# Decode of four attention layers: six blocks of output-weight rows laid out unevenly over the partitions

## The chip, the cores and the metric

The kernel runs on one core of a Trainium2 chip. The metric is the time of one execution in microseconds on the device; the median of three runs before the change is 1974.63 us (1973.94 to 1975.71).

## The reference

One token goes through four layers, A, B, A, B. Each layer normalises the token, makes a query of 32 heads of 192 from it, attends over a cache of 8192 keys and values a head, and projects the 32 x 192 = 6144 results back to 640 with the output weights `wo`, whose result is added to the token.

```python
def _A_ref(x, k_cache, v_cache, wq, wo):        # _B_ref is the same with its own arrays
    q = ((x @ wq).reshape(B, Sq, Hq, Dh)).transpose(0, 2, 1, 3)
    scores = jnp.einsum("bhqd,bhkd->bhqk", q, k) * (Dh ** -0.5)
    p = _softmax(scores, axis=-1)
    o = jnp.einsum("bhqk,bhkd->bhqd", p, v)
    return o.transpose(0, 2, 1, 3).reshape(B, Sq, Hq * Dh) @ wo
x = A_x
x = x + _A_ref(_layernorm(x), A_k_cache, A_v_cache, A_wq, A_wo)
x = x + _B_ref(_layernorm(x), B_k_cache, B_v_cache, B_wq, B_wo)
x = x + _A_ref(_layernorm(x), A_k_cache, A_v_cache, A_wq, A_wo)
x = x + _B_ref(_layernorm(x), B_k_cache, B_v_cache, B_wq, B_wo)
```

## The kernel before

The kernel reads 845 MB, nearly all of it caches, and reads the caches once for each layer. Layers are counted from 0 here (layers 0 and 2 are A, 1 and 3 are B). A layer's 32 heads are taken as 16 pairs. The keys of a pair, and its values, are 6.29 MB each: one head on 64 partitions, the other on the other 64, 49,152 bytes a partition. They land in halves or whole in a pool of eight slots (`slot`, line 129).

For a pair the order of the work is: VectorE multiplies the keys in place by the query (line 744), TensorE sums the products with matmuls against the identity (lines 72, 762), VectorE and ScalarE make the softmax (802 to 817), TensorE multiplies by the values (859, 72), and `gather` (869) picks each head's row out of the result: VectorE 883 and 885, a matmul (899), and two ScalarE copies with the softmax's divisor (908) into `orow`, one row of SBUF on one partition.

**A block of output weights** belongs to five pairs (`PAIRS_W`): 5 x 384 = 1920 of the 6144 rows of `wo`, 640 wide, 1280 bytes a row. `transfer` (line 439) loads it with one transfer of 128 partitions with `NW` = 15 consecutive rows each (lines 492, 493). A layer has three such blocks, called (layer, 0), (layer, 1), (layer, 2) here, and one more pair's rows at its end. After the fifth pair of a block:

- `columns` (718) turns `orow` from a row into 15 columns of 128: column i takes every 15th element from i on, with a one-row matmul into `TB` (722), and one ScalarE copy puts the columns into `oT` (725).
- `project_row` (688) multiplies: for each of the 15 columns, two matmuls, one for each half of the 640 outputs, with the column as weights (695). They add up in one accumulator (`YR`). Its last matmul is what frees the block's slot (`freed[n]`).

**The order.** `steps` is the order of the work, `plan` that of the loads (lines 262 to 324). All loads are issued by SyncE in the order of `plan`; `before` names whose work must be done before a load may overwrite a slot, and `transfer` waits for these (`free`). A load that has to wait holds up all that follow it on SyncE. `ahead` (504) hands SyncE the loads whose conditions are known. In layers 0 and 1, places are fixed: the block has the third slot of a ring, which keys of a later pair use next. In layers 2 and 3 `allot` (357) gives each load the slots that come free first; in layer 2 the values of the pair after a block get one of their halves in the block's slot, so this half's issue waits for the end of `project_row`. A transfer's end is a semaphore that counts to 16, one for each DMA engine.

Of the kernel before, what the change touches and what calls it, by code (L numbers as in the profile page):

```python
# [4 lines left out]
ACT = mybir.ActivationFunctionType  # L5
# [77 lines left out]
def build(nc, A_x, A_k, A_v, A_wq, A_wo, B_x, B_k, B_v, B_wq, B_wo, out):  # L83
# [21 lines left out]
    OI = PD // P  # L105
    WB = [[], [6], [], [7]]
    NB = [sum(b) for b in WB]
    VLAST = [0, 2, 0, 4]
    G = 4
    VK = 8  # L110
# [6 lines left out]
    with ExitStack() as ctx:  # L117
# [311 lines left out]
        def block_rows(l, i=None):  # L429
# [3 lines left out]
            x = 0 if l != 1 else TS // 2 if i is None else -(NW - NB[l]) * D  # L433
            return t[:, x + a * D:x + b * D], a, b

        def quarters(n):
            return n[0] == "v" and n[2:] == (NPAIR - 1, 1) and NB[n[1]] > 0

        def transfer(n):
            l = n[1]  # L440
            o = ORDER[l]
            w = W[l % 2]
            free = [freed[b] for b in before[n]]
            if n[0] in ("wol", "woe"):
                r0 = o["wol"] * PD
                a, b = (0, OI) if l < 3 else (0, OI - 1) if n[0] == "wol" else (OI - 1, OI)
                return SP.op(lambda s: s.dma_start(
                    last_rows(l)[:, a * D:b * D], w["wo"][r0:r0 + PD].rearrange("(p i) n -> p (i n)", p=P)[:, a * D:b * D]),
                    *free, sem=semOL if n[0] == "wol" else semOE, inc=16)
            if n[0] == "wob":  # L450
                r0 = o["wo"][2] * PD
                t, a, b = block_rows(*n[1:])
                return SP.op(lambda s: s.dma_start(
                    t, w["wo"][r0:r0 + PAIRS_W * PD].rearrange("(p i) n -> p (i n)", p=P)[:, a * D:b * D]),
                    sem=(semOB, semOE)[n[2]], inc=16)
            if n[0] == "vq":
                n = ("v", l, NPAIR - 1, 1)
            if n[0] in ("kh", "kp"):
                h = 2 * pair(l, 0)
                i = n[3] if n[0] == "kp" else 0  # L460
                a, b, to = PIECE[i]
                r = w["k"][0, h:h + 2].rearrange("h (p j) d -> (h p) (j d)", j=J)[:, a:b]
                return SP.op(lambda s: s.dma_start(to, r), *free, sem=[semVQ, *semR, semS[A_WQ]][i], inc=16)
            i = place[n]
            t = slot[i]
            if n[0] in "kv":
                h = 2 * pair(l, n[2])
                r = w[n[0]][0, h:h + 2].rearrange("h (p j) d -> (h p) (j d)", j=J)
                if quarters(n):
                    x = TS - VLAST[l] * TS // 8  # L470
                    if n in landed:
                        return SP.op(lambda s: s.dma_start(t[:, x:], r[:, TS + x:]), sem=semVQ, inc=16)
                    return SP.op(lambda s: s.dma_start(t[:, 0:x], r[:, TS:TS + x]), *free, sem=semS[i], inc=16)
                if whole(*n[:3]):
                    if n[3] == 1:
                        return landed[n[:3] + (0,)]
                    f = lambda s: s.dma_start(pool[:, i * TS:(i + 2) * TS], r)
                else:
                    x = TS // 2 if n == ("k", 0, 0, 0) else 0
                    f = lambda s: s.dma_start(t[:, x:], r[:, n[3] * TS + x:(n[3] + 1) * TS])  # L480
            elif n[0] == "wq" and l < 2:
                a, b = (0, DC) if l == 0 else (0, DC - 1) if n[2] == 0 else (DC - 1, DC)
                f = lambda s: s.dma_start(pool[:, i * TS:i * TS + (b - a) * QW],
                                          w["wq"].rearrange("(p c) n -> p (c n)", c=DC)[:, a * QW:b * QW])
            elif n[0] == "wq":
                c0, k = Q_PARTS[n[2]]
                f = lambda s: s.dma_start(
                    wq_rows(l, n[2]),
                    w["wq"][:, o["q1"] * PD:o["q1"] * PD + QC[l]].rearrange("(p c) n -> p c n", c=DC)[:, c0:c0 + k, :])
            else:  # L490
                r0 = o["wo"][n[2]] * PD
                t, _, k = block_rows(l) if n[2] == 2 else (t[:, 0:NW * D], 0, NW)
                f = lambda s: s.dma_start(t, w["wo"][r0:r0 + PAIRS_W * PD].rearrange("(p i) n -> p (i n)", p=P)[:, 0:k * D])
            return SP.op(f, *free, sem=semS[i], inc=16)

        def need(n):
# [51 lines left out]
        def layer(l, ev_z, ev_true):  # L548
# [139 lines left out]
            def project_row(n, w, o, ev_o):  # L688

                t3 = w.rearrange("p (i n) -> p i n", n=D)  # L690
                k = t3.shape[1]
                PE.wait(ev_o, need(n), last["YB"])
                for i in range(k):
                    for h in range(2):
                        e = PE.op(lambda t, i=i, h=h, f=l < 3 and n[2] == 0 and i == 0, fin=n == last_row and i == k - 1: t.matmul(  # L695
                            YR[32 * h:32 * h + 1, :], lhsT=o[:, i:i + 1], rhs=t3[:, i, h * HD:(h + 1) * HD], start=f, stop=fin,
                            skip_group_check=True), signal=(i == k - 1 and h == 1), bank=YBu)
# [17 lines left out]
                y_first[0] = False  # L715
                return e

            def columns(k):

                PE.wait(last["row_written"], last["TT"], ev_const)  # L720
                for i in range(k):
                    e = PE.op(lambda t, i=i: t.matmul(TB[:, i:i + 1], lhsT=orow[:, i:k * P:k], rhs=one_b[96:97, :],
                                                      start=True, stop=True), signal=(i == k - 1), bank=TBu)
                last["orow"] = freed[n] = e
                last["TT"] = AC.op(lambda a: a.activation(oT[:, 0:k], TB[:, 0:k], ACT.Copy),  # L725
                                   e, last["oT"], bank=TBu)

            ev_S, ev_s, ev_p, ev_O, ev_l = {}, {}, {}, {}, {}

# [139 lines left out]
            def gather(p):  # L869
# [31 lines left out]
                if end:  # L901
                    last["TTn"] = last["TO"] = AC.op(
                        lambda a: a.activation(oTl[:], TB[:, 0:OI], ACT.Copy, scale=rl[:, 0:1]), e, ev_rl, last["oTl"], bank=TBu)
                else:
                    o0 = (pair(l, p) - ORDER[l]["wo"][p // PAIRS_W]) * PD
                    AC.wait(e, ev_rl, last["orow"], last["qbc"])
                    for h in range(2):
                        last["TO"] = last["row_written"] = AC.op(lambda a, h=h: a.activation(  # L908
                            orow[:, o0 + h * DH:o0 + (h + 1) * DH], TB[64 + 32 * h:65 + 32 * h, C_O:C_O + DH], ACT.Copy,
                            scale=rl[64 + 32 * h:65 + 32 * h, h:h + 1]), bank=TBu)  # L910

            q_ready = False
            for n in [n for n in steps if n[1] == l]:
# [22 lines left out]
                    q_rows(n[2])  # L936
                    q_ready = n[2] == 2 or q_ready
                elif n[0] == "wc":
                    columns(NW)
                    last["oTw"] = last["TT"]  # L940
                elif n[0] == "wo":
                    t, _, k = block_rows(l) if n[2] == 2 else (slot[place[n]][:, 0:NW * D], 0, NW)
# [95 lines left out]
```

## Time and profile before

| | |
|---|---|
| median of three runs | 1974.63 us |
| span of the profiled execution, first to last instruction | 1972.3 us |
| read from HBM | 845.22 MB, 429 GB/s over the span |
| mean granted TensorE clock | 0.842 |
| DMA issues of a block (line 493) | 12, of 1.3 to 2.5 MB, 15.9 to 38.4 us from issue to landing |
| issue and last landing of the six blocks that change, us | (0,0) 148.16, 174.74; (0,1) 299.40, 326.13; (1,1) 804.24, 830.64; (2,0) 1144.18, 1161.94; (2,1) 1297.18, 1313.64; (3,0) 1602.01, 1635.30 |

Times within the execution count from its first instruction. The profile's page gives, for each engine, its busy time and share of the span; a row of 40 digits shows the busy share in 40 equal slices, 9 for 90% or more. "q1" is the queue of the loads that SyncE issues; "q8" and "q14" bring the program's instructions. The chain of waits goes back from an instruction to what released it; in it, a line has start, duration, and what ran. In the timeline a line has start, duration, engine, line of the kernel, what it writes and reads, and in brackets how long the engine had been idle and what ended that.

### The profile page before, as it was taken

How to read it: one execution, taken by the hardware profiler on the slowest of the kernel's cores; microseconds unless marked ns; L12 is line 12 of the kernel's file. 1: busy time of each engine (PE TensorE's matmuls, PEld its weight loads, DVE VectorE, ACT ScalarE, POOL GpSimd, SP SyncE). 2: the span in 40 equal slices, each digit the busy share in tenths (PEclk: the TensorE clock that was granted, in tenths of full speed). 3: DMA queues.
4: the chain of work that ended last, by engine and by line, in shares of the span. 5: the costliest groups of instructions: out<-in, count | busy, mean ns of one | idle time of the engine just before them, and what ended most of it. 6: DMA issues, size and time to landing. Idle time of an engine off the chain costs nothing.

```text
span 1972.3 us, 13138 instructions
## 1 busy us (share of the span) xinstructions
PE 1425.8 (72%) x8648; PEld 138.3 (7%) x2789; DVE 1204.7 (61%) x910; ACT 146.2 (7%) x465; POOL 4.6 (0%) x25
## 2 busy tenths in 40 slices
PE   4788777886578888788786675776676667657658
PEld 0000000000200100000020000000002001000001
DVE  3566665667256566665856565665664765665756
ACT  0000000000000000000000000000000100000000
POOL 0000000000000000000000000000000000000000
PEclk9898998998689888988887777777787878777779
DMA  9999999999999999999999999999999999999998
GB/s 414 430 431 432 431 434 431 436 425 427 437 429 431 430 428 432 433 429 432 431 419 436 426 430 434 429 431 430 431 430 427 433 432 436 432 433 432 431 432 369
DMA packets 27245, 846.07 MB, mean 429 GB/s; under 512 B 3122, under 2 KB 3252, under 8 KB 4148
## 3 DMA queue, kind: packets, MB, share of 16 engines
q1 hardware_dynamic: 27044, 845.23, 99.7%
q8 instruction: 45, 0.74, 0.2%
q14 instruction: 12, 0.10, 0.0%
q10 hardware_dynamic: 144, 0.00, 0.0%
HBM read 845.22 MB, written 0.00 MB: 429 GB/s over the span
## 4 chain that ended last, share of the span: by engine, by line
DMA 58%; PE 22%; DVE 19%; ACT 1%; issue 0%; SPq 0%
DMA pool<-in_B_k_cache_dram 24%; DMA pool<-in_A_v_cache_dram 16%; DMA pool<-in_A_k_cache_dram 16%; DVE pool L744 14%; PE S L72 13%; PE OY L72 4%; PE OY L859 3%; DMA pool<-in_B_wo_dram 2%; DVE OY L883 1%; DVE acc L885 1%; DVE s_sb L802 1%; DMA pool<-in_B_v_cache_dram 1%; PE OY L695 1%; ACT p_sb L817 1%; DVE pool L776 1%
## 5 line engine op out<-in xcount | busy, mean ns | idle before, releaser
L744 DVE TENSOR_TENSOR pool<-pool,q_sb 128x3584 bf16<-128x3584 bf16 (+3 forms) x460 | 844.4, 1907 | 189.5 <-DMA pool<-in_B_k_cache_dram 99.1
L72 PE MATMUL S<-pool,ident 128*128 128x512 bf16 x3004 | 758.8, 407 | 37.9 <-DVE pool L744 34.5
L883 DVE TENSOR_TENSOR OY<-OY,small 128x1536 f32<-128x1536 f32 x60 | 106.0, 1767 | 253.4 <-PE OY L72 253.2
L72 PE MATMUL OY<-pool,p_sb 128*16 128x512 bf16 x1920 | 211.9, 530 | 0.0
L72 PE MATMUL S<-ident 128*128 128x512 bf16 x775 | 185.3, 387 | 0.0
L859 PE MATMUL OY<-pool,p_sb 128*16 128x512 bf16 (+1 forms) x1216 | 148.0, 510 | 42.0 <-DMA pool<-in_A_v_cache_dram 34.6
L802 DVE TENSOR_REDUCE s_sb<-S 128x128 f32<-128x1024 f32 x63 | 77.2, 1225 | 110.4 <-PE S L72 110.4
L899 PE MATMUL TB<-acc,small 128*33 128x192 f32 x120 | 39.8, 423 | 135.6 <-DVE acc L885 135.6
L885 DVE TENSOR_REDUCE acc<-OY 128x192 f32<-128x1536 f32 x60 | 105.5, 1758 | 2.0
L762 PE MATMUL S<-pool,ident 128*128 128x512 bf16 x66 | 33.7, 511 | 95.8 <-DVE pool L744 95.8
L908 ACT ACTIVATE rows<-TB,small 1x192 bf16<-1x192 f32 x120 | 49.5, 412 | 571.4 <-PE TB L899 569.9
L589 ACT ACTIVATE q_sb<-QM 128x192 bf16<-128x192 f32 x59 | 19.5, 330 | 928.9 <-PE QM L645 928.9
L807 PE MATMUL QM<-ident,m_bf 128*64 128x64 bf16 x128 | 14.0, 216 | 86.4 <-DVE m_bf L804 86.4
L817 ACT ACTIVATE p_sb<-s_sb,small 64x128 bf16<-64x128 f32 x128 | 55.7, 435 | 194.4 <-DVE small L811 193.6
L832 PE MATMUL TB<-small,ones 128*33 128x2 f32 x120 | 14.4, 190 | 74.1 <-ACT p_sb L817 74.1
L873 DVE RECIPROCAL small<-TB 33x2 f32<-33x2 f32 x64 | 11.2, 175 | 88.9 <-PE TB L832 72.6
L645 PEld LDWEIGHTS QM<-rows,one_b 1*64 1x64 bf16 x118 | 6.1, 100 | 720.5 <-issue 720.5
L859 PEld LDWEIGHTS OY<-pool,p_sb 128*16 128x16 bf16 (+1 forms) x1216 | 36.3, 110 | 199.0 <-issue 148.0
L530 PE MATMUL S<-ident 128*128 128x512 bf16 x80 | 33.8, 422 | 17.2 <-DMA pool<-in_A_k_cache_dram 10.9
L695 PE MATMUL OY<-pool,oT 128*1 128x320 bf16 x330 | 38.1, 408 | 2.4 <-ACT oT L725 2.2
L811 DVE TENSOR_REDUCE small<-QM 128x1 f32<-128x64 f32 x64 | 14.4, 225 | 31.3 <-PE QM L807 31.3
L899 PEld LDWEIGHTS TB<-acc,small 128*33 128x33 f32 x120 | 9.6, 124 | 272.3 <-DVE acc L885 272.3
(87 smaller groups left out, 270.2 us busy)
## 6 DMA issues: line engine op xcount, KB each, us to landing
pool<-in_B_v_cache_dram SPq DMA_DIRECT2D x28, 6144.0 KB, 27.6
pool<-in_A_v_cache_dram SPq DMA_DIRECT2D x27, 6144.0 KB, 23.8
pool<-in_B_k_cache_dram SPq DMA_DIRECT2D x27, 6144.0 KB, 22.2
pool<-in_A_k_cache_dram SPq DMA_DIRECT2D x35, 3072.0 KB, 19.9
pool<-in_A_k_cache_dram SPq DMA_DIRECT2D x13, 6144.0 KB, 21.0
pool<-in_A_v_cache_dram SPq DMA_DIRECT2D x10, 3072.0 KB, 13.5
pool<-in_B_k_cache_dram SPq DMA_DIRECT2D x10, 3072.0 KB, 20.3
pool<-in_A_wo_dram SPq DMA_DIRECT2D x6, 2400.0 KB, 18.4
```

The costliest lines, as they stand in the source:

```text
L72: return t.add_instruction(mybir.InstMatmult(name=t.bass.get_next_instruction_name(), engine=mybir.EngineType.PE, ins=[t.lower_ap(rhs), t. ...
L530: t.matmul(SP_[0][:, :], lhsT=ident[:], rhs=ident[:].unsqueeze(1).broadcast_to([P, 4, P]), start=True, stop=True)
L695: e = PE.op(lambda t, i=i, h=h, f=l < 3 and n[2] == 0 and i == 0, fin=n == last_row and i == k - 1: t.matmul(YR[32 * h:32 * h + 1, :], lhs ...
L744: e = DV.op(lambda v, d0=d0, QD=QD, kin=kin, kout=kout, n=n: v.tensor_tensor(kout[:, :, d0:d0 + QD], kin[:, :, d0:d0 + QD], q_sb[qi][:, d0 ...
L762: t.matmul(S[:, :], lhsT=ident[:], rhs=k3[:, :, d0:d0 + R], start=d0 == 0, stop=fin)),
L802: lambda v: v.tensor_reduce(s[:], S_[:].rearrange("p (j r) -> p j r", r=R), AX.X, ALU.add),
L817: ev_p[p] = AC.op(lambda a, h=h, r=r: a.activation(p_sb[par][r, :, h], s[r, :], ACT.Exp, bias=negm[par][r, 0:1], accum_out=l_col[par][r, h ...
L859: t.matmul(o, lhsT=x, rhs=y, start=f, stop=fin) if c == 0 else
L883: e = DV.op(lambda v: v.tensor_tensor(o3, o3, pick[:, 0:VK].unsqueeze(2).broadcast_to([P, VK, DH]), ALU.mult), bank=Ou)
L885: e = DV.op(lambda v: v.tensor_reduce(acc[:], O.rearrange("p (i d) -> p d i", d=DH), AX.X, ALU.add), e, bank=Ou)
L899: e = PE.op(lambda t: t.matmul(TB[64:97, C_O:C_O + DH], lhsT=half33, rhs=acc[:], start=True, stop=True), bank=TBu)
L908: last["TO"] = last["row_written"] = AC.op(lambda a, h=h: a.activation(orow[:, o0 + h * DH:o0 + (h + 1) * DH], TB[64 + 32 * h:65 + 32 * h, ...
```

## The change

Six blocks, (0,0), (0,1), (1,1), (2,0), (2,1) and (3,0), are laid out in another way; the other six stay. Of the block's 1920 rows, the first 128 x 14 = 1792 go to the 128 partitions, 14 consecutive rows each, with one transfer. The last 128 rows go to 32 partitions, four consecutive rows each: partitions 0 to 15 and 32 to 47, with two further transfers of 16 partitions. The change takes partitions 0 to 3 and 32 to 35 for those of DMA engine 0, the next four each for those of engine 1, and so on to engine 3; the source of each of the two transfers is led by a dimension of four, one step an engine, with the engine's four partitions inside it. All three transfers count on the slot's semaphore, and the last one's event is the block's.

The rest follows the layout. `orow` holds the last 128 results in the order of the partitions (the copy of the block's last head is cut in two, the second with a permuting pattern). `columns` makes 14 columns of 128 and, for each of the two groups of partitions, four columns of 16; three copies take them to `oT`, which is 18 wide. `project_row` runs over 14 columns on all partitions, then four on partitions 0 to 15, then four on 32 to 47: 22 pairs of matmuls in the place of 15, with a wait for its own earlier matmuls before the third part.

```diff
+    UNEVEN = {(l, b): (14, ((4, 4),)) for l, b in ((0, 0), (0, 1), (1, 1), (2, 0), (2, 1), (3, 0))}
...
-        oT = sb("oT", [P, NW], BF16)
+        oT = sb("oT", [P, NW + 3], BF16)
...
+        def uneven(l, b):
+
+            m, groups = UNEVEN.get((l, b), (NW, ()))
+            r, c, out = P * m, m, []
+            for k, x in groups:
+                out.append((r, c, k, x))
+                r, c = r + 8 * k * x, c + x
+            assert r == PAIRS_W * PD
+            return m, out, c
...
+                if n[1:] in UNEVEN:
+                    m, groups, _ = uneven(*n[1:])
+                    e = SP.op(lambda s: s.dma_start(t[:, 0:m * D], rows_of[0:P * m].rearrange("(p i) n -> p (i n)", p=P)),
+                              *free, sem=semS[i], inc=16)
+                    for r, c, k, x in groups:
+                        for h in range(2):
+                            to = t[32 * h:32 * h + 4 * k, c * D:(c + x) * D]
+                            r4 = rows_of[r:r + 8 * k * x].rearrange("(b a i) n -> b a i n", b=4, i=x)[:, h * k:(h + 1) * k]
+                            e = SP.op(lambda s, to=to, r4=r4: s.dma_start(to, r4.rearrange("b a i n -> a b (i n)")), sem=semS[i], inc=16)
+                    return e
...
             def project_row(n, w, o, ev_o):
...
+                todo = [(slice(0, P), i) for i in range(t3.shape[1])]
+                if n[0] == "wo" and n[1:] in UNEVEN:
+                    m, groups, _ = uneven(*n[1:])
+                    todo = todo[:m] + [(slice(32 * g, 32 * g + 4 * k), i) for g in range(2) for _, c, k, x in groups for i in range(c, c + x)]
                 PE.wait(ev_o, need(n), last["YB"])
-                for i in range(k):
+                for j, (a, i) in enumerate(todo):
+                    end = j + 1 == len(todo) or a.start < todo[j + 1][0].start
+                    if a.start and not todo[j - 1][0].start:
+                        PE.wait(e)
                     for h in range(2):
...
-                            YR[32 * h:32 * h + 1, :], lhsT=o[:, i:i + 1], rhs=t3[:, i, h * HD:(h + 1) * HD], start=f, stop=fin,
-                            skip_group_check=True), signal=(i == k - 1 and h == 1), bank=YBu)
+                            YR[32 * h:32 * h + 1, :], lhsT=o[a, i:i + 1], rhs=t3[a, i, h * HD:(h + 1) * HD], start=f, stop=fin,
+                            skip_group_check=True), signal=end and h == 1, bank=YBu)
...
-            def columns(k):
+            def columns(b):
 
+                m, groups, k = uneven(l, b)
+                todo = [(slice(0, P), i, orow[:, i:m * P:m]) for i in range(m)]
+                for r, c, ke, x in groups:
+                    for g in range(2):
+                        a = r + 4 * g * ke * x
+                        todo += [(slice(32 * g, 32 * g + 4 * ke), c + i, orow[:, a + i:a + 4 * ke * x:x]) for i in range(x)]
...
+                parts = [(slice(0, P), 0, m)] + [(slice(32 * g, 32 * g + 4 * ke), c, c + x) for _, c, ke, x in groups for g in range(2)]
+                for a, c0, c1 in parts:
+                    last["TT"] = AC.op(lambda s, a=a, c0=c0, c1=c1: s.activation(oT[a, c0:c1], TB[a, c0:c1], ACT.Copy), bank=TBu)
...
+                        moves = [(a0, a1, None)] if a1 < PAIRS_W * PD or not groups else [(a0, groups[0][0], None)] + [
+                            (r, r + 8 * k * x, x) for r, _, k, x in groups]
+                        for r0, r1, x in moves:
...
+                            last["TO"] = last["row_written"] = AC.op(lambda a, h=h, to=to, of=of: a.activation(
+                                to, of, ACT.Copy, scale=rl[64 + 32 * h:65 + 32 * h, h:h + 1]), bank=TBu)
```

More of the change, by code (lines that the diff above doesn't have):

```diff
@@ L716, in to_columns @@
                 return e
-            def columns(k):
+            def columns(b):
[5 more added lines that the diff above has]
+                        todo += [(slice(32 * g, 32 * g + 4 * ke), c + i, orow[:, a + i:a + 4 * ke * x:x]) for i in range(x)]
                 PE.wait(last["row_written"], last["TT"], ev_const)
-                for i in range(k):
-                    e = PE.op(lambda t, i=i: t.matmul(TB[:, i:i + 1], lhsT=orow[:, i:k * P:k], rhs=one_b[96:97, :],
-                                                      start=True, stop=True), signal=(i == k - 1), bank=TBu)
+                for j, (a, i, w) in enumerate(todo):
+                    e = PE.op(lambda t, a=a, i=i, w=w: t.matmul(TB[a, i:i + 1], lhsT=w, rhs=one_b[96:97, :],
+                                                                start=True, stop=True), signal=(j == len(todo) - 1), bank=TBu)
                 last["orow"] = freed[n] = e
-                last["TT"] = AC.op(lambda a: a.activation(oT[:, 0:k], TB[:, 0:k], ACT.Copy),
-                                   e, last["oT"], bank=TBu)
+                AC.wait(e, last["oT"])
+                parts = [(slice(0, P), 0, m)] + [(slice(32 * g, 32 * g + 4 * ke), c, c + x) for _, c, ke, x in groups for g in range(2)]
+                for a, c0, c1 in parts:
+                    last["TT"] = AC.op(lambda s, a=a, c0=c0, c1=c1: s.activation(oT[a, c0:c1], TB[a, c0:c1], ACT.Copy), bank=TBu)
             ev_S, ev_s, ev_p, ev_O, ev_l = {}, {}, {}, {}, {}
@@ L906, in gather @@
                     AC.wait(e, ev_rl, last["orow"], last["qbc"])
+                    _, groups, _ = uneven(l, p // PAIRS_W)
                     for h in range(2):
[L908 to L910 removed]
+                        a0, a1 = o0 + h * DH, o0 + (h + 1) * DH
+                        moves = [(a0, a1, None)] if a1 < PAIRS_W * PD or not groups else [(a0, groups[0][0], None)] + [
+                            (r, r + 8 * k * x, x) for r, _, k, x in groups]
+                        for r0, r1, x in moves:
+                            to, of = orow[:, r0:r1], TB[64 + 32 * h:65 + 32 * h, C_O + r0 - a0:C_O + r1 - a0]
+                            if x is not None:
+                                to = to.rearrange("p (a b i) -> p b a i", b=4, i=x)
+                                of = of.rearrange("p (b a i) -> p b a i", b=4, i=x)
+                            last["TO"] = last["row_written"] = AC.op(lambda a, h=h, to=to, of=of: a.activation(
+                                to, of, ACT.Copy, scale=rl[64 + 32 * h:65 + 32 * h, h:h + 1]), bank=TBu)
             q_ready = False
@@ L938, in layer @@
                 elif n[0] == "wc":
-                    columns(NW)
+                    columns(n[2])
                     last["oTw"] = last["TT"]
                 elif n[0] == "wo":
-                    t, _, k = block_rows(l) if n[2] == 2 else (slot[place[n]][:, 0:NW * D], 0, NW)
+                    t, _, k = block_rows(l) if n[2] == 2 else (slot[place[n]][:, 0:uneven(*n[1:])[2] * D], 0, uneven(*n[1:])[2])
                     if l == 3 and n[2] == 0:
```

6 lines of the change are left out of this document (3 added, 3 removed).

## The prediction

> **What bounds the kernel.** I read the profile's page first: busy rows, the row of the DMA engines, the queues, the chain.
>
> ```profile
> span 1972.3 us, 13138 instructions
> PE 1425.8 (72%) x8648; PEld 138.3 (7%) x2789; DVE 1204.7 (61%) x910; ACT 146.2 (7%) x465; POOL 4.6 (0%) x25
> ...
> DMA  9999999999999999999999999999999999999998
> ...
> q1 hardware_dynamic: 27044, 845.23, 99.7%
> q8 instruction: 45, 0.74, 0.2%
> q14 instruction: 12, 0.10, 0.0%
> ...
> DMA 58%; PE 22%; DVE 19%; ACT 1%; issue 0%; SPq 0%
> ```
>
> The 16 DMA engines are full from the first slice to the last; no compute engine is. So the time is that of the DMA engine that finishes last: its bytes, what else it carries, and its gaps. Next I read the trace's sixteen landings of each transfer (each engine reports its own share). First landing, then all sixteen lags behind it, us:
>
> ```
> 381.71: 0 .03 .25 .38 .47 .48 .88 1.36 2.00 2.01 2.06 2.10 2.18 2.23 2.44 2.58
> 396.23: 0 .03 .26 .39 .48 .49 .89 2.00 2.02 2.07 2.11 2.20 2.24 2.45 2.59 2.93
> 1963.97: 0 .10 .14 .63 .72 .91 1.33 2.94 3.32 3.83 4.08 4.15 4.67 5.16 5.30 5.44
> ```
>
> Between such transfers of 6.29 MB an undisturbed engine needs 14.53 us for its 393,216 bytes, 27.06 bytes per ns, and all sixteen the same. What separates them is single jumps: from line one to line two the engine at 1.36 goes to 2.93, in a stretch with one 16 KB instruction fetch (q8, at 391.6). So **a fetch of TensorE's code costs the engine that carries it 1.57 us**. The 45 fetches repeat their durations with period eight: eight engines take them in turn, five or six each, and eight carry none. The last line, of the last weight rows, shows the outcome: seven engines ahead, nine 2.9 to 5.4 us behind. The leaders' lead would be larger had they not run dry where loads were issued late (at 470 it falls by 1.0, from 1013 to 1025 by 1.0, at 690, 720 and 872 by about 0.3 each): in all some 8.5 us by the end.
>
> Third, the places where a load waits for a changed block. Of the six blocks, the two of layer 2 (0-based) matter, since there the next half of values goes into the slot of the block. The chain of waits around the first, then the SyncE queue, then the second block's matmuls:
>
> ```profile
> 1131.56 24.65 DMA pool<-in_A_v_cache_dram
> ...
> 1166.04 0.41 ACT rows L908
> 1166.45 0.03 issue
> 1166.48 0.42 ACT rows L908
> 1166.90 0.05 issue
> 1166.94 1.09 PE TB L722 x15
> 1168.03 0.02 issue
> 1168.06 0.19 ACT oT L725
> 1168.25 0.04 issue
> 1168.29 3.77 PE OY L695 x30
> 1172.07 0.32 PE S L762
> ```
> ```profile
> 1172.11 5.80 SPq L480 DMA_DIRECT2D pool<-in_A_v_cache_dram  x2
> ```
> ```profile
> 1319.23 4.16 PE L695 MATMUL OY<-pool,oT 128*1 128x320 bf16 x30 [0.27 <-ACT oT L725]
> ```
>
> The chain is rigid from the landing of the values (1156.22) to the issue at 1172.11, the moment the projection (L695) lets go of the slot. The transfer issued before that one lands on its engines from 1174.15 to 1176.56, so the issue is 2.05 us ahead of the first engine's running dry and 4.45 ahead of the last's. How much is needed? The key load issued at 460.70 was 1.02 ahead and came 1.03 late (8.30 instead of 7.27): 2.05. At 703.16: 1.57 ahead, 0.77 late: 2.34. At 1172.11 itself: 0.09 late: 2.14. I take **2.1 us from issue to first byte**; the highest seen is 2.8. At 1323.43 the slowest engine has 4.83 (1328.26).
>
> **The bytes.** Before, each engine carries 8 x 15 x 1280 = 153,600 bytes of a block. After: 143,360 on twelve, 143,360 + 40,960 = 184,320 on four. At 27.06 bytes per ns: twelve save 0.378 us a block, four lose 1.135. Six blocks: -2.27 and +6.81, 9.08 between them, beside the lead of 8.5. The largest possible gain is 2.27 us. Pieces are 5,120 bytes; the last rows, in pieces of 1,280, took 0.41 instead of 0.38 us, so under 10% more of 1.5 us a block, 0.1 us, on the four.
>
> **Two more loads on SyncE a block.** Issues in a row stand 0.37 to 0.47 us apart: +0.9. Behind them the queue's next instruction is a load issued 5.8 us (1150.03 after 1144.18) or more later: nothing. Without that cover, 0.9 us later issue. The block's own landing, up to 1.2 us later on four engines, is hidden: landed at 1161.94, used at 1168.29.
>
> **The compute chain of a block**, per step: one more row copy (L908), 0.42; seven more column matmuls (22 for 15) at 1.09/15 = 0.073, 0.51; two more copies of 0.19 (L725), 0.38; the projection 44 matmuls for 30, at 3.77/30 = 0.126 each 1.76 (second block 4.16/30, 1.94). New: TensorE waits once for its own matmul before the second row group, which no row shows; a matmul of L695 lasts 0.30 to 0.51, so between 0 and 0.5, taken 0.3. Sum **3.37 us, 3.55 in the second**. Bounds: the 16-row matmuls as cheap as the one-row ones (0.073), 2.5; or 0.2 each, beyond which halves that now overlap would have to stop overlapping, 4.5. Queued behind on TensorE are the next pair's score matmuls, for whom the VectorE products are ready 1 us earlier anyway.
>
> In layers 0 and 1 this lies in a gap: the projection ends at 187.8, 337.8 and, with its turn to columns, 843.7, and the next keys land at 189.3, 340.7 and 845.3. It overruns these by at most 2 us, and the loads that follow have 5.4 us or more ahead of the slowest engine, against 2.1. Layer 3's loads are over 10 us ahead. If that cover went, each would cost up to 3.4.
>
> In layer 2 it isn't hidden. Positions of the slowest engine against before: three blocks in layers 0 and 1, -1.13. First block: issue at 1172.11 - 1.13 + 3.37 = 1174.35, the transfer ahead ends at 1176.56 - 1.13 - 0.38 = 1175.05, that is 0.70 ahead where 2.1 is needed: 1.40 idle, position -0.11. And the idle levels all engines: a saved lead is gone, so the next fetches (1234.6, 1291.4) make a new last one, +1.57, where before they fell on engines with lead. Values then land at +1.46. Second block: issue 1323.43 + 1.46 + 3.55 = 1328.44, first bytes at 1330.54 against 1328.26: position +2.28, all level again. From there the slowest gains 3.0 on a clean engine before (2.5 to 5.5), two fetches, as after. Layer 3's block: -0.38. **Sum +1.9 us**. The four: level at +2.28, +1.14, perhaps two small fetches, stay within the 3.0 of the others. Against the profiled execution that is 1974.2; runs have a median of 1974.63, 2.3 over this span, so **1976.5**. With chain bounds 2.5 and 4.5 the sum moves twice the difference: +0.2 to +4.1 (1974.8 to 1978.8).
>
> **Rivals.**
> - **The four are not the free ones** (slower). The trace doesn't say which engine is which; it says eight of sixteen carry code. If the four, or one of them, do, then up to layer 2 they are at +3.4 and with the first block +4.5, no idle; the others resume at +4.35, one is hit (5.9), second block 1323.43 + 5.9 + 3.55 + 2.1, +6.7; layer 3's block +1.1: +7.8; where the one hit trailed a round, 1.57 or more less, and with two rounds +4.5. Taken +6: 1980.6. It decides if one of the four is within 1.5 us of the last. For: half the engines are laden. Against: if the free eight are neighbours, half of the aligned fours are free. Were code fetches free for the DMA engines, all sixteen would be level and the four last in the same way, 6 x 1.135 = +6.8 and no idle to hide it; the jump from 1.36 to 2.93 leaves that 0.02 of this case's chance.
>
> The Trainium skill, Runtime: NRT & Kernel Launch, section "Instruction fetch mechanics", speaks for such a level start: it has the crossing of a 16 KiB boundary "mostly hidden". The trace agrees for TensorE, whose chain shows no stall for code, and not for the DMA engine, at 1.57 us.
>
> - **The chain is hidden**, because the added matmuls cost under 1.5 us in all: no idle in layer 2, the gain stays, -1 to -2.3: 1973. Against: every added step has a row.
> - **The extra rows don't go to four engines**, but over all: bytes level as before, only the chain: first block 3.37 - 2.35 = +1.0, hit +2.6, second block +3.4, no gain: 1978. No run here shows a transfer of 16 partitions.
>
> The Trainium skill, DMA: Bandwidth & Descriptors, section "Why a DMA increments its semaphore by 16 and not by 1", speaks against that last one: a source led by a dimension of four uses the four lowest-numbered engines; by it that rival falls away; no run here shows it.
>
> **Chances.** Forecast 0.55, laden four 0.30, hidden chain 0.10, spread rows 0.05. 0.2% of 1974.6 is 3.9 us, about what a measurement of this kernel can tell from no change. Faster by more would need more than the 2.27 there is: 0.03. Slower: most of the laden case (0.27) and the top of the forecast's range: 0.32. Same: 0.65. The range, 1973.0 to 1982.0, takes in most of the hidden chain and of the laden four; the forecast's own is 1974.8 to 1978.8.
>
> **What would show it.** Of the landings of a block's extra loads, only four report late, and these four are seen among the leaders (right) or the last (laden). The chain from L908 to the projection's end grows by 3.4 us. The values behind the two blocks of layer 2 are issued with under 2.1 us ahead, and the sixteen landings behind them stand within 0.5 us. At the end the spread is near 3 to 4 instead of 5.4 us. Wrong it would be if the values' issue kept its distance, or the chain grew by less than 2 or more than 5 us.

## The result, and the profile after

| | before | after |
|---|---|---|
| median of 8 runs each, us | 1974.38 (1973.94 to 1976.73) | 1979.65 (1978.89 to 1982.19) |
| ratio, 95% interval | | 1.0024 (1.0013 to 1.0034) |
| span of the profiled execution, us | 1972.3 | 1978.1 |

The kernel is 5.3 us slower in the medians and 5.8 in the spans. The ratio, 1.0024, is small, but its interval leaves out no change. The time lies inside the range of the prediction, 3.1 us above its forecast and 1.0 below the time of its first rival.

The page of the changed kernel, the lines shown of before:

```profile
span 1978.1 us, 13420 instructions
...
PE 1433.0 (72%) x8774; PEld 141.5 (7%) x2915; DVE 1204.7 (61%) x910; ACT 148.5 (8%) x483; POOL 4.6 (0%) x25
...
DMA  9999999999999999999999999999999999999998
...
q1 hardware_dynamic: 27284, 845.23, 99.6%
q8 instruction: 46, 0.75, 0.2%
q14 instruction: 12, 0.10, 0.0%
...
DMA 58%; PE 22%; DVE 18%; ACT 1%; issue 0%; SPq 0%
```

Same bytes, same bound: the DMA engines, full in every slice. 126 more matmuls (6 blocks by 14, and 6 by 7 columns) add 7.2 us to TensorE's busy time, one more code fetch (q8) is there; neither is where the end is decided.

The chain of waits through the first block of layer 2 (start, us, what):

```profile
1167.71 0.41 ACT rows L953
1168.12 0.03 issue
1168.15 0.57 ACT rows L953 x2
1168.72 0.05 issue
1168.77 1.22 PE TB L756 x22
1169.99 0.02 issue
1170.01 0.23 ACT oT L762 x2
1170.24 0.02 issue
1170.26 0.17 ACT oT L762
1170.43 0.04 issue
1170.48 5.07 PE OY L723 x36
1175.55 0.04 issue
1175.59 1.23 PE OY L723 x8
1176.81 0.54 PE S L798
```

From the first row copy (L953, L908 before) to the issue of the values at 1176.85 it is 9.14 us, before 6.07: +3.07. At the second block 9.13 for 6.44: +2.69. The parts: row copies +0.15, column matmuls +0.13, copies of `oT` +0.23, projection 6.33 for 3.77, +2.56 (second block 6.34 for 4.16).

Where the time went is read best from positions: when the slowest engine of a transfer lands, changed kernel minus before, profiled runs (e1, e2, e4, e5 and e9 are experiments, below). Where an experiment's change has not begun yet, its profile mostly agrees with that of the kernel before to about 0.3 us. The largest differences there are 0.84 in these rows (e2, the values before (2,0)) and 1.56 between them (e2 from 1031 on: behind a code fetch at 1022 its last engine alone is later). Single differences under 1 us therefore say little:

```
transfer, last landing before     after    e1    e2    e4    e5    e9
keys behind (0,0)       189.28   -0.06   0.08  0.15  0.28 -0.26 -0.01
keys behind (0,1)       340.67    0.81   1.47  0.20  1.13 -0.43  0.06
keys behind (1,1)       845.32    1.26   1.25  0.12  1.57 -0.30  0.25
values before (2,0)    1156.22    2.08   2.20  0.84  2.40  1.66  0.25
keys behind (2,0)      1176.56    3.26   3.05  1.98  3.58  1.65 -0.16
third half behind      1198.46    5.54   3.06  1.95  3.62  2.72  3.61
keys behind (2,1)      1328.26    5.22   3.42  2.94  4.61  2.54  4.66
third half behind      1350.23    7.34   3.36  2.89  4.63  4.64  4.59
last weight rows       1969.41    5.82   3.07  1.67  4.85  3.62  4.67
```

Up to the first block of layer 2, where the prediction had a gain of 1.1 us, 2 are lost (1.26 by the keys behind (1,1)); another 5 around its two blocks; and 1.5 come back by the end. The sixteen landings of three transfers around the first block of layer 2 in the changed kernel (first landing, then all lags, us) show how:

```
keys      1176.23: 0 .01 .07 .07 .23 .40 .48 .55 1.29 1.51 1.64 1.64 1.69 1.70 1.73 3.58
values    1185.95: 0 .08 .13 .13 .22 .23 .32 .34 .39 .44 .51 .62 .68 .71 .82 1.16
keys      1201.23: 0 .17 .21 .23 .23 .30 .39 .67 .73 .82 .92 .97 1.04 1.06 1.26 2.77
```

In the first line one engine alone is last, 1.85 us behind the next: the fifteen others wait for nobody and gain nothing by it. Then the values are issued late (1176.85), the fifteen run dry and the line shrinks to 1.16. Then, with a code fetch at 1195.7 between, one engine is 1.5 us behind again, and this time it is lost time for the end.

The row of TensorE's clock explains one part of the lateness. Before, then after: the projection of the first block, the score matmuls behind it up to the issue of the second half of the values, then the same of the second block:

```profile
1168.30:1172.10 3.80, 3.80 (x31) 1.82 (x31) 2.83 (x2) 0.00 (x0) 0.00 (x0) 0.57 1.01 433
1172.10:1177.60 5.50, 5.41 (x24) 0.00 (x0) 4.96 (x4) 0.00 (x0) 0.00 (x0) 1.00 1.00 419
...
1319.20:1323.40 4.20, 4.17 (x31) 1.88 (x31) 2.43 (x2) 0.00 (x0) 0.00 (x0) 0.50 1.01 433
1323.40:1329.60 6.20, 6.16 (x24) 0.03 (x1) 5.66 (x4) 0.00 (x0) 0.00 (x0) 0.86 0.99 420
```
```profile
1170.50:1176.80 6.30, 6.24 (x45) 2.37 (x45) 4.25 (x3) 0.00 (x0) 0.00 (x0) 0.50 0.91 390
1176.80:1183.90 7.10, 7.10 (x29) 0.04 (x1) 6.58 (x5) 0.00 (x0) 0.00 (x0) 0.80 0.89 346
...
1324.80:1331.10 6.30, 6.24 (x45) 2.35 (x45) 4.88 (x3) 0.00 (x0) 0.00 (x0) 0.50 0.89 382
1331.10:1339.20 8.10, 8.10 (x26) 0.03 (x1) 7.58 (x6) 0.00 (x0) 0.00 (x0) 0.66 0.92 367
```

A row is a stretch, its length, the busy time of PE, PEld, DVE, ACT, POOL, the granted clock, the share and the GB/s of the DMA engines. The clock is 0.50 in the longer projection (before 0.57 and 0.50), and behind it TensorE gets 0.80 and 0.66 for 1.00 and 0.86. The second half of the values waits for score matmuls, so its issue slips further, by 1.2 and 1.9 us more than the first half's (4.74 and 5.95 us late against before at the first block, 7.70 and 9.58 at the second). The last column shows the DMA engines short of work: 346 to 390 GB/s where it was 419 to 433.

This low clock doesn't belong to the longer projection as such. At the first block of layer 2 the same 44 matmuls took 4.73 us at a granted clock of 0.73 in e2 and 5.16 us at 0.67 in e5, with 1.00 behind them in both, and 6.34 us at 0.50 in e8. Up to 1.6 us of the chain's price thus change from run to run.

### The profile page after: what moved, and what is told of

It reads as the page before. It is cut to its first block, busy times and chain, and to the rows that moved or that the text cites. A ratio compares the mean times of both kernels' runs of the same rounds, so it can differ in the third digit from the quotient of the medians.

```text
span 1978.1 us, 13420 instructions
## 1 busy us (share of the span) xinstructions
PE 1433.0 (72%) x8774; PEld 141.5 (7%) x2915; DVE 1204.7 (61%) x910; ACT 148.5 (8%) x483; POOL 4.6 (0%) x25
## 4 chain that ended last, share of the span: by engine, by line
DMA 58%; PE 22%; DVE 18%; ACT 1%; issue 0%; SPq 0%
DMA pool<-in_B_k_cache_dram 24%; DMA pool<-in_A_k_cache_dram 17%; DMA pool<-in_A_v_cache_dram 15%; DVE pool L780 14%; PE S L72 13%; PE OY L72 4%; PE OY L895 3%; DMA pool<-in_B_wo_dram 2%; DVE OY L919 1%; DVE acc L921 1%; PE OY L723 1%; DVE s_sb L838 1%; DMA pool<-in_B_v_cache_dram 1%; ACT p_sb L853 1%; DVE pool L812 1%; PE S L798 0%
## 5 line engine op out<-in xcount | busy, mean ns | idle before, releaser
L72 PE MATMUL OY<-pool,p_sb 128*16 128x512 bf16 x1920 | 206.4, 518 | 0.0
L953 ACT ACTIVATE rows<-TB,small 1x192 bf16<-1x192 f32 (+2 forms) x126 | 50.4, 404 | 566.6 <-PE TB L935 565.1
L723 PE MATMUL OY<-pool,oT 128*1 128x320 bf16 (+1 forms) x414 | 50.5, 416 | 4.0 <-ACT oT L762 3.5
```

Source lines behind the costliest of these rows:

```text
L72: return t.add_instruction(mybir.InstMatmult(name=t.bass.get_next_instruction_name(), engine=mybir.EngineType.PE, ins=[t.lower_ap(rhs), t. ...
L723: e = PE.op(lambda t, a=a, i=i, h=h, f=l < 3 and n[2] == 0 and j == 0, fin=n == last_row and j + 1 == len(todo): t.matmul(YR[32 * h:32 * h ...
L953: last["TO"] = last["row_written"] = AC.op(lambda a, h=h, to=to, of=of: a.activation(to, of, ACT.Copy, scale=rl[64 + 32 * h:65 + 32 * h, h ...
```

## The experiments

Two theories to begin with, the extra bytes (A) and the late issues of layer 2 (B). All kernels below but e7 are the changed one with the edit shown.

**e1, only layers 0 and 1 uneven.**

```diff
-    UNEVEN = {(l, b): (14, ((4, 4),)) for l, b in ((0, 0), (0, 1), (1, 1), (2, 0), (2, 1), (3, 0))}
+    UNEVEN = {(l, b): (14, ((4, 4),)) for l, b in ((0, 0), (0, 1), (1, 1))}
```


> Only the three blocks of layers 0 and 1 are uneven. Theory A (bytes too early: at 170 and 325 us no engine has more than 2.9 us of lead over the last, and the four are given 1.51 each time): the four become the last ones, the kernel is 1.5 to 2.5 us slower than before, and the values ahead of the first block of layer 2 land about 2 us later than before, as in the changed kernel (+2.08). Theory B (the bytes are harmless, all the loss is the idle time in layer 2): 1.1 us faster than before.

Measured 1977.17 for 1974.7, ratio 1.0012 (1.0003 to 1.0021). The slowest engine is 2.20 us later before layer 2 and 3.07 at the end. As A: half of the loss comes from blocks that the prediction had as a gain.

**e2, only layer 2 uneven.**

```diff
-    UNEVEN = {(l, b): (14, ((4, 4),)) for l, b in ((0, 0), (0, 1), (1, 1), (2, 0), (2, 1), (3, 0))}
+    UNEVEN = {(l, b): (14, ((4, 4),)) for l, b in ((2, 0), (2, 1))}
```


> Only the two blocks of layer 2 are uneven. Theory A: the longer chain costs what is left of it behind the 4.45 and 4.83 us that the slowest engine has, and one code fetch falls on levelled engines: 2 to 3.5 us slower than before, because the four have lead by then. Theory B: 5 us slower or more, the whole of the loss.

1976.77, ratio 1.0010 (1.0001 to 1.0019): B's 5 us fall. At the two blocks the slowest engine goes from +0.84 to +1.98 and from 1.76 to 2.97: 1.14 and 1.21, the full price of the extra bytes (worked out: 1.135), so one of the four was last. This goes against A's reason, by which the four have lead by then. The values of the first block were issued 4.25 us ahead of the slowest engine's end of the transfer before (1174.29 for 1178.54), those of the second 3.81, and it doesn't run dry. e1 and e2 together, 2.5 and 2.1 us, make up 4.6 of the 5.3.

**e3, the extra rows over all sixteen engines.** Two loads of 16 partitions, each partition's rows on another engine; same compute as the change.

```diff
-                            r4 = rows_of[r:r + 8 * k * x].rearrange("(b a i) n -> b a i n", b=4, i=x)[:, h * k:(h + 1) * k]
-                            e = SP.op(lambda s, to=to, r4=r4: s.dma_start(to, r4.rearrange("b a i n -> a b (i n)")), sem=semS[i], inc=16)
+                            r4 = rows_of[r + 4 * h * k * x:r + 4 * (h + 1) * k * x]
+                            e = SP.op(lambda s, to=to, r4=r4: s.dma_start(to, r4.rearrange("(p i) n -> p (i n)", i=x)), sem=semS[i], inc=16)
...
-                            if x is not None:
-                                to = to.rearrange("p (a b i) -> p b a i", b=4, i=x)
-                                of = of.rearrange("p (b a i) -> p b a i", b=4, i=x)
```


> All six blocks uneven in layout and in compute, but the two extra loads of a block are spread over all sixteen engines, one partition each, so that every engine carries the 153,600 bytes of before. Only the chain is left. Theory A: no loss up to layer 2 (position within 0.5 us of before), then the idle time: 2 to 3.5 us slower than before, and 2 to 3 faster than the changed kernel. Theory B: as slow as the changed kernel, +5.

1986.96, ratio 1.0058 (1.0046 to 1.0071): +12.3 us, which neither expected. The reason is in the loads themselves. The slowest engine is 7.36 us later than in the kernel before at the values before (2,0) and 9.56 at the keys behind that block, 9.34 and 11.58 around (2,1): 2.2 us more a block, though each engine carries the bytes of before. Its two pieces of 5,120 bytes should need 2 x 5,120 / 27.06 = 0.38 us, as the fifteenth row did. The trace of e3 over the stretch in which the small loads end at (2,0), then the same at (2,1) (columns as above):

```profile
1166.50:1172.00 5.50, 2.33 (x24) 0.15 (x4) 3.09 (x2) 0.00 (x0) 0.00 (x0) 0.81 0.96 359
...
1320.00:1326.00 6.00, 2.47 (x28) 0.14 (x4) 3.45 (x2) 0.00 (x0) 0.00 (x0) 0.78 0.95 338
```

The engines are busy (0.96, 0.95) and move only 359 and 338 GB/s: the packets are slow. Those of 5,120 bytes take 0.252 us in the median and up to 0.65, for 0.196 in the changed kernel. Those of other loads beside them are slow too: from 1164 to 1167 packets of 17,920 bytes take up to 1.48 us and packets of 24,576 up to 1.96, where the changed kernel has medians of 0.67 and 0.92 around this block. So e3 says nothing on A and B. What differs from the change is that sixteen engines instead of four write into the same sixteen partitions, each from another piece of the source; that the writing is what hinders them is likely, and no run separates it from the reading. The Trainium skill, DMA: Bandwidth & Descriptors, section "The descriptor swizzle", bears on it: it puts partitions 0 to 15 and 32 to 47 on four of sixteen ports. By that an estimate is 20,480 bytes on a port, 0.76 us for each small load instead of 0.19, or 1.1 us more a block; the trace agrees in kind and shows more, 2.2.

**e4, the bytes alone**: the loads of the change, the compute of before.

```diff
-                if n[0] == "wo" and n[1:] in UNEVEN:
-                    m, groups, _ = uneven(*n[1:])
+                if False:
...
-                m, groups, k = uneven(l, b)
+                m, groups, k = NW, (), NW
...
-                    _, groups, _ = uneven(l, p // PAIRS_W)
+                    groups = ()
...
-                    t, _, k = block_rows(l) if n[2] == 2 else (slot[place[n]][:, 0:uneven(*n[1:])[2] * D], 0, uneven(*n[1:])[2])
+                    t, _, k = block_rows(l) if n[2] == 2 else (slot[place[n]][:, 0:NW * D], 0, NW)
```


> The loads of the changed kernel, the compute of before (15 columns a block; it leaves out the three last rows of each of the 32 partitions and multiplies stale data on the other 96, so the output is not the reference's). Only the bytes are left. Theory A: the position ahead of layer 2 is +2 as in the changed kernel, no idle time in layer 2, in all 2 to 4 us slower than before. Theory B: 2.3 us faster than before.

1978.42, ratio 1.0018 (1.0009 to 1.0027): +3.7 us, as A. With no longer chain at all and as many code fetches as before (45), 2.40 us are gone before (2,0), and the blocks of layer 2 take 1.18 and 1.20 more.

**e5, the chain alone**: the loads of before, the compute of the change.

```diff
-                if n[1:] in UNEVEN:
+                if False:
                     m, groups, _ = uneven(*n[1:])
```


> The counterpart of e4: the loads of the kernel before, the compute of the changed one (22 column matmuls, 44 projection matmuls, the extra row copies and oT copies). It leaves out part of the computation: of the last row of the six blocks only 32 partitions are multiplied, and the extra columns multiply what lies in the slot. No byte moves otherwise. Measured so far: from the values' landing to the issue the chain takes 2.66 us more at the first block of layer 2 and 2.36 at the second; the slowest engine before has 4.45 and 4.83 us ahead there, so 1.8 and 2.5 are left where some 2.1 to 2.3 are needed. Theory A (the loss is the bytes', on an engine that is among the last, and the chain takes only what the gaps had over): at most 0.5 us of idle for the slowest engine at the first block, none at the second, leaders idle 2 to 5 us, so the levelled engines may be hit by a fetch: +0 to +2 us at the end, sum of e4 (+3.7 to +4.9) and this near the change's +5 to +5.8. Theory B (the recorded prediction's pricing of the chain: any delay of the issue levels the engines and each fetch then makes a new last one): +2.6 after the first block, +3.4 at the end (2.5 to 4.5), and e4 and this sum to 7 or more, more than the change itself.

1977.81, ratio 1.0014 (1.0005 to 1.0022): +3.1 us, +3.6 in the span. The median lies above A's 0 to 2 (the interval, about 1 to 4.3 us, reaches into it) and near the 3.4 of B, the recorded prediction's pricing. But 1.67 us of it are there before (2,0), with the bytes of before and ahead of any late issue of layer 2, and neither theory has them. The last step to them, 0.94 us, comes in the transfer in which an 8 KB fetch lies (q14, at 1139.2): it sets back the engine that is last already, while the same fetch in the kernel before, at 1138.1, leaves the last engine where it was.

At layer 2 itself the trace shows B's mechanism. The values of the first block are issued at

```profile
1175.58 5.61 SPq L491 DMA_DIRECT2D pool<-in_A_v_cache_dram  x2
```

3.47 us later than before and 2.62 ahead of the slowest engine, which therefore doesn't run dry; but the first engine is set back from +0.43 to +3.20, the spread falls from 3.62 to 0.77, and the next jump on a levelled engine is a loss: +1.07 by 1198 (a fetch at 1193.8), and at the second block +2.1. By the medians, bytes and chain alone, 3.7 and 3.1, make more than the change's 5.3: it seems that each eats a part of the other's.

**e6, only layer 3 uneven**, both blocks (the change has one), where loads are issued 10 us and more ahead.

```diff
-    UNEVEN = {(l, b): (14, ((4, 4),)) for l, b in ((0, 0), (0, 1), (1, 1), (2, 0), (2, 1), (3, 0))}
+    UNEVEN = {(l, b): (14, ((4, 4),)) for l, b in ((3, 0), (3, 1))}
```


> The uneven lay only in the two blocks of layer 3 (one of them is not in the change), where loads are issued over 10 us ahead and no chain can matter; the full result. Engines 0 to 3 then carry 2 x 1.135 us more and the twelve others 2 x 0.378 less, at the time when the leaders' lead is largest (five engines are over 4 us ahead of the last at the end, before). If all four are leaders, the last engine gains 0.76: -0.8 us (0 to -0.8). Theory A (one of the four is among the last, as e4 and the landings of the change show): +1.1 to +2.3 us, and the end spread grows from 5.4 to 6 or more. If the bytes do not matter at all: within 0.3 us.

1974.23, ratio 1.0000 (0.9991 to 1.0009): no difference to be told, and A's +1.1 to +2.3 fell. At (3,0) the slowest engine goes forward by 0.38, the whole saving of the twelve, so in this run none of the four was within 1.5 us of the last there; e7, below, has engine 3 at 0.61 at that block. How far an engine lags thus differs by about 1 us from run to run. In the profile the first engine gains 0.70, as twelve engines with less to carry should, and the spread at the end grows from 5.44 to 6.27, as A expected. But the engine that is last behind (3,1), +0.58 us against before, meets no jump in the 170 us that are left (its lag stays at 6.3), while in the kernel before the spread still grows by 0.7. At the end they are equal, -0.18. What bytes on a late engine cost at the end thus depends on whether the next fetches fall on it; that its share of these differs from kernel to kernel is seen, what assigns them is not.

**e7, which engine is which.** The kernel before, with eight loads of two numbers behind each block, of 1 to 8 partitions.

```diff
+        def probing():
+            probes[0] += 1
+            for k in semP:
+                last_probe[k] = SP.op(lambda s, k=k: s.dma_start(probe[k * (k - 1) // 2:k * (k + 1) // 2, 0:2], B_wo[0:k, 0:2]), last_probe.get(k), sem=semP[k], inc=16)
```


> The kernel before, and after each block of output-weight rows eight loads of two numbers, of 1 to 8 partitions, each with a semaphore of its own: a load of k partitions goes to k engines, so the reports that load k+1 has and load k lacks are those of one more engine, and which of the first eight engines lead or lag at each block can be read. 72 extra small loads or so cost each of these engines a few us in all: the time is not compared (+1 to +8 us). Theory A: of engines 0 to 3 one at least is within 0.5 us of the last engine at layer 2, and stays so. Theory B (the four are leaders, held back only by idle): all four are over 1.5 us ahead of the last at layer 2 and over 2.9 at the end.

**e8, the same probes in the changed kernel.**

> The changed kernel with the probing loads of e7 behind each block of output-weight rows. In the kernel before, e7 put engine 3 at 0.97, 1.36, 1.45, 0.57 and 0.38 us ahead of the last engine at the blocks (0,0), (0,1), (1,1), (2,0) and (2,1), engines 0 and 1 between 1.0 and 2.3, engine 2 between 2.0 and 3.7. An uneven block sets each of the four back by 1.135 and the others forward by 0.378: 1.51 against each other. Theory A (the loss is engine 3's): in the changed kernel engine 3 is the last of all engines behind (0,0), (0,1), (1,1) and both blocks of layer 2 (0 to 0.3 us before the last report), engines 0 and 1 0.5 to 1.5 us ahead of it, engine 2 always ahead of these two or beside them. Theory B (the recorded forecast: the four are free engines): all four lie beside each other, and ahead of most others wherever leaders had not run dry.

The load of k partitions is reported by k engines, and each report recurs 0.15 to 0.2 us later in the list of load k + 1, with one new beside it: at (2,0) in e7 1159.52; 1159.67 1159.70; 1159.56 1159.86 1159.89; 1159.74 1160.04 1160.09 1161.27. The newcomer of the fourth, engine 3, is 1.2 us behind the three others. How far each of the four is ahead of the last engine, us (the last landing of the block, plus the 0.19 that a report takes, less the newcomer's report):

```
block    before (e7): engine 0    1    2    3    changed (e8): 0    1    2    3
(0,0)                1.86 2.09 2.06 0.97                1.24 1.12 1.16 0.00
(0,1)                1.71 1.49 2.29 1.36                0.71 0.13 1.06 0.00
(1,1)                2.27 2.04 3.73 1.45                0.95 0.35 2.58 0.00
(2,0)                2.32 2.17 2.29 0.57                1.75 1.62 2.04 0.00
(2,1)                1.61 1.05 2.02 0.38                1.50 0.02 1.71 1.19
(3,0)                1.80 1.67 2.74 0.61                0.93 0.01 1.40 0.69
end                  1.23 1.08 3.32 0.67                0.94 0.01 2.52 1.32
```

As A in the main: before, engine 3 is near the last at every block (0.57 and 0.38 in layer 2, where A had said within 0.5), 0 and 1 keep a lead that doesn't grow, and only engine 2 pulls ahead, as do 4 and 7 of the first eight (4.4 and 5.0 at the end). An uneven block sets the four back by 1.135 + 0.378 = 1.51 against the others, and engine 3 had that much nowhere. In the changed kernel it is the last of all at the first four blocks, and from the second of layer 2 on, against A, engine 1. (One run each: 1973.66, where the probes cost nothing that can be told, and 1982.48, 2.8 above the changed kernel, which wasn't to be compared.) The Trainium skill, DMA: Bandwidth & Descriptors, section "Why a DMA increments its semaphore by 16 and not by 1", says that such a load uses the lowest-numbered engines of the core; the nested lists agree.

**e9, engine 3 spared**, one uneven block.

```diff
-    UNEVEN = {(l, b): (14, ((4, 4),)) for l, b in ((0, 0), (0, 1), (1, 1), (2, 0), (2, 1), (3, 0))}
+    UNEVEN = {(2, 0): (14, ((3, 4), (4, 1)))}
...
-        oT = sb("oT", [P, NW + 3], BF16)
+        oT = sb("oT", [P, NW + 4], BF16)
```


> One uneven block, the first of layer 2, with engine 3 spared: of the 128 rows that are laid apart, 96 go to engines 0 to 2 and 32 to engines 0 to 3, so engine 3 carries what it carried before, engines 0 to 2 1.51 us more, the other twelve 0.378 less. Two more columns than the change (24 for 22), the full result. To be compared with e2 at the same block, where the slowest engine went from +0.84 to +1.98 us against the kernel before (+1.14). Theory A (engine 3 was the last): the slowest engine goes forward or stays, -0.4 to +0.1, since engines 0 to 2 lead by 2.2 to 2.3 there and lose 1.9. Theory B (it is the four's bytes or the added loads themselves, whichever engine carries them): +1.1 to +1.5, as in e2 or more. The time itself is near the kernel before with one delayed issue: +0.5 to +2 us by both.

The slowest engine goes from +0.25 to -0.16 at the block, where e2 went from +0.84 to +1.98. The forward step, 0.41, is the saving of an engine that isn't one of the four (0.378). So the bytes harm nobody here, where engine 3 does not carry them, as A says. It is one run, and where engine 3 stood in it was not read; with e6 in mind it supports A and does not settle it alone. The time missed its expectation, 1978.79 in one run beside 1975.01: with 24 columns the projection takes 6.9 us, the issue is at

```profile
1176.60 8.52 SPq L491 DMA_DIRECT2D pool<-in_A_v_cache_dram  x2
```

4.5 us late, after the last landing of the transfer ahead (1176.40) and not before it; all sixteen engines run dry, +3.61, and the next fetch makes it 4.7. One late issue, with all engines level behind it, costs 4.7 us in the profile, where the whole change costs 5.8.

No version that beats the kernel before came out of this; none of the nine is measurably faster.

## Why the prediction came out as it did

The time lies in its range, but not by its likeliest case, whose own range ended at 1978.8. The range given, 9 us wide, was drawn to take in the rivals as well, so that the time lies in it is in good part luck. In the order of its steps:

- **The bound**, 14.53 us a transfer and sudden jumps where code is fetched: as said. The jump behind the first block of layer 2 is 1.51 us (1.57 said).
- **The bytes**, 0.378 less on twelve, 1.135 more on four: right in size, 1.14 to 1.21 in e2 and e4. And only four engines report the extra loads, so the rival of rows spread over all engines is out.
- **"Three blocks in layers 0 and 1, -1.13"** is the step that failed. It took the four for engines with a lead that pays for the extra bytes; measured +2.08, and +2.40 with the bytes alone (e4). Of the 2.08, 1.26 are there behind (1,1); the other 0.8 come by 1156, in a stretch without an uneven block, in which engine 3's lead falls from 1.45 to 0.57 us in e7 (e2, with nothing changed there yet, loses 0.7 in it too). Engine 3 was 0.97, 1.36 and 1.45 us ahead of the last at these blocks (e7) and needed 1.51. The prediction set 9.08 us of extra bytes beside a lead of 8.5, but that is the lead at the end: at (0,0) and (0,1) the earliest engine of all is only 2.2 and 2.6 us ahead of the last in the kernel before, and two blocks within 150 us take 3.0.
- **The laden four**, the first rival, decides "if one of the four is within 1.5 us of the last": it was. Its course runs 1.2 to 1.3 us too high, +3.4 for 2.08 up to layer 2, +4.5 for 3.26 with the first block; its 4.5 to 7.8 at the end hold the measured 5.82. By the trace at hand it was the likelier case: when half of sixteen are laden, four that are all free are the rarer.
- **The chain**, +3.37 and +3.55: measured 3.07 and 2.69. The projection's share was too small (2.06 said with the added wait, 2.56 measured at the first block, where the clock was 0.50 for 0.57), the row copies, columns and `oT` copies too large (1.31 for 0.51). That the sum comes out near is partly luck: at the clock of e2 the projection takes only 0.96 us more than before. That the chain is hidden falls with e5, where a late issue and the fetch behind it set the slowest engine back by 1.07 at the first block and 2.1 at the second.
- **The idle of layer 2.** Predicted 1.40 us for the slowest engine at the first half. It had none there: it was so far back that the issue, 4.74 us later than before, still came 2.97 us ahead of it, and 2.34 at the second block. The fifteen others ran dry as predicted, with landings 1.16 and 0.39 us apart behind the two blocks for the 0.5 said, and the levelled engines then met a fetch as predicted. Not in the sum: the second halves of the values, late through the lower clock, +0.78 and +0.98. At the first block this half was issued 2.4 to 3.6 us before the engines ended the half ahead and still landed 0.7 to 1.0 late on all of them; why the usual 2.1 to 2.8 were not enough there stays open.
- **The growth to the end**, "same as before": the slowest engine gained 1.5 on before (7.34 to 5.82). The spread at the end, 3.47, is in the 3 to 4 that was said. It doesn't tell the forecast from the rival, nor does the chain; the position before layer 2 and the distance of the issue do. So does the prediction's own first sign: the four that report late are seen among the last (e8), not among the leaders.

The sum, +1.9, against 5.8 in the spans: 3.2 of the difference are there before (2,0).

## What to carry to other kernels

Before bytes are moved to some DMA engines because engines have slack, find out which engines these are, and how much lead they have at that very transfer, not at the end: a few loads of 1 to 8 partitions with semaphores of their own show it, at no cost that e7 shows, and for that run: another (e6) differs by about 1 us. A lead of the others is no reserve, since the slowest engine alone sets the end; and the lead is gone the first time that a transfer is issued late, after which every disturbance counts. A chain on which an issue waits is to be priced with what runs behind it on the same engine, and at more than one clock.

## What was not expected of the hardware

Small loads into sixteen neighbouring partitions by sixteen engines take several times as long as their bytes and slow the packets beside them (e3: 2.2 us a block on top of 0.38). And a stretch of matmuls has no fixed price: 44 of them with weights of one column, at the first block of layer 2, took 6.33 us at a granted clock of 0.50 in the changed kernel, 5.16 at 0.67 in e5 and 4.73 at 0.73 in e2, and the full matmuls behind them got 0.80, 1.00 and 1.00. The Trainium skill, TensorE: Matmul & The Clock Gate, section "What's actually happening", has the clock at full after some 3.4 us of sustained work; the trace agrees in e2 and e5, where it rises to full within the stretch, and not in the changed kernel, where 6.3 us of these matmuls do not release it. What decides between the two stays open.
